# Moving the second look at layer 0's weights from layer 1 to block 1 of layer 0, with layer 1's first tiles loaded behind it

## The chip, the cores and the metric

One core of a Trainium2 chip runs the program. The metric is the device time of one execution in microseconds (us). TensorE (PE) multiplies matrices, VectorE (DVE) and ScalarE (ACT) do the elementwise work, GpSimd (POOL) a little of it, and SyncE (SP) issues all the DMAs of this program in one queue. Each engine runs its instructions in the order in which they stand in its own list, and waits at an instruction until what it depends on is there.

## The reference

Attention with sink tokens and a window, then two feed-forward layers, each with its own weights, which come as 64-bit floats:

```python
def _moe_ref(x, w_in, w_out):            # layer 0
    h = x @ w_in                          # [1536, 512] @ [512, 2048]
    sp = np.where(h > 20.0, h, np.log1p(np.exp(np.minimum(h, 20.0))))
    return (h * np.tanh(sp)) @ w_out      # [1536, 2048] @ [2048, 512]

def _moe2_ref(x, w_in, w_out):           # layer 1
    h = x @ w_in
    return (h * np.clip(h + 3.0, 0.0, 6.0) / 6.0) @ w_out

def reference(...):
    x = attention(q, k, v, n_sink, window)    # [2, 8, 768, 64] -> [1536, 512]
    return _moe2_ref(_moe_ref(x, ...), ...)
```

## The kernel before

The 1536 tokens are 12 units of 128, grouped into three blocks of four (`BLOCKS`). Attention for the first two blocks is computed ahead and beside layer 0's first steps; attention for the third block (units 8 to 11, `last`) runs as side work beside layer 0's block 1. The matmuls of the layers run in steps. In layer 0 a step takes two of the 16 slices f of the hidden dimension for one block: `up` multiplies the input by w_in into h (24 matmuls of 512 columns, two halves), a chain on ScalarE and VectorE makes the activation, and `down` multiplies by w_out (24 matmuls). `down` comes one step late (`LAG = 1`). Every value is kept as a high and a low float16 half: the chain ends with the high half of g on ScalarE (L748) and the low half on VectorE (L749), whose input e VectorE writes just before (L744). In order, layer 0 runs block 0 (stage 0), block 1 (stage 1) and block 2 (stage 2), eight steps each; layer 1 follows with steps of four slices, multiplied by Strassen's scheme in `up2` and `down2`.

Weights come in 16 tiles for each layer. `fetch_w` loads one tile (w_in and w_out parts, 512 KB each) into `raw`, of which there are two buffers (`STB = 2`). `gen_decode` turns a tile into float16 halves: on VectorE two operations into y (L210, L211), one into p (L212), then splits (L250, L268) and, for a pair of layer 1's tiles, four sums t (L260 to L263). y has one buffer. Layer 0's 16 tiles are decoded in stage 0, layer 1's in stage 2 and at the start of layer 1, a pair in most steps (`PAIRS`). When a tile's y and p are made, `load_w` fetches the next tile in the sequence `wseq` (layer 0's, then layer 1's), so two tiles are always ahead.

The second look (`gen_check`) loads layer 0's tiles once more, two ahead, and for each one masks the exponents on VectorE (`exponents`, L184) and sums them on ScalarE (L188). The sums only serve the test, at the end, of whether the fast path was allowed.

The pieces of side work (attention, decoding, look) are handed out by `hook`, four times in a step. A scheduler then orders the instructions of each engine, and may move them ahead where it expects their inputs; a look is marked to keep its place. Setting `budget["chk"]`, `CHECK = 7` lets the look begin at the eighth stage, in layer 1, once `raw_t` is empty, that is when all of layer 1's tiles are decoded. In the loop over steps, before stage 2, `att_side.until` hands out what is left of attention, and `open_second` frees attention's buffers and takes them for layer 1's.

Of the kernel before, what the change touches and what calls it, by code (L numbers as in the profile page):

```python
# [29 lines left out]
def attention_moe_moe2(  # L30
# [13 lines left out]
    nc = tc.nc  # L44
# [4 lines left out]
    KF = DFF // 128  # L49
# [109 lines left out]
    wseq = [(layer, f) for layer in range(2) for f in range(KF)]  # L159
    wsrc = ((w1_in, w1_out), (w2_in, w2_out))  # L160
    nload = [0]

    def fetch_w(layer, f):
        wi, wo = wsrc[layer]
        t = st_p.tile([128, 2, 512, 2], I32, tag="raw", name="raw")
        nc.sync.dma_start(
            out=t[:, 0].rearrange("p (k f) t -> p k (f t)", k=KD),
            in_=wi[:, f * 256:(f + 1) * 256].rearrange("(k p) f -> p k f", p=128),
        )
        nc.sync.dma_start(out=t[:, 1].rearrange("p f t -> p (f t)"), in_=wo[f * 128:(f + 1) * 128, :])  # L170
        return t

    def load_w():
        if nload[0] >= len(wseq):
            return
        layer, f = wseq[nload[0]]
        nload[0] += 1
        raw_t[layer, f] = fetch_w(layer, f)

    def exponents(idx, t, pin=False):  # L180

        y = dec_p.tile([128, 1024], I32, tag="y", name="y").bitcast(I16)[:, 0:1024]
        top = t.rearrange("p f t -> p (f t)").bitcast(I16).rearrange("p (f t) -> p f t", t=4)[:, :, 3]
        look = nc.vector.tensor_scalar(out=y, in0=top, scalar1=0x7800, scalar2=0x3800, op0=ALU.bitwise_and, op1=ALU.bitwise_xor)  # L184
        if pin:
            tc.keep_in_program_order(look)
        yy = y.bitcast(I32)
        nc.scalar.activation(out=yy, in_=yy, func=AF.Copy, accum_out=wchk[:, idx:idx + 1])  # L188

    def gen_check():  # L190


        ahead = []
        for f in range(KF + 2):
            if f > 1:
                exponents(f - 2, ahead.pop(0).rearrange("p a f t -> p (a f) t"), True)
            if f < KF:
                ahead.append(fetch_w(0, f))
            yield
            yield  # L200

    def gen_decode(idx):
        layer, f = wseq[idx]
        t = raw_t.pop((layer, f)).rearrange("p a f t -> p (a f) t")
        halves = t.rearrange("p f t -> p (f t)").bitcast(I16).rearrange("p (f t) -> p f t", t=4)
        y = dec_p.tile([128, 1024], I32, tag="y", name="y")
        yh = y.bitcast(I16).rearrange("p (f t) -> p f t", t=2)
        p = (late["p"] if layer == 1 else dec_p).tile([128, 1024], I32, tag="p", name="p")

        nc.vector.tensor_scalar(out=yh[:, :, 1], in0=halves[:, :, 3], scalar1=-0x800, scalar2=-0x800, op0=ALU.bitwise_and, op1=ALU.bitwise_xor)  # L210
        nc.vector.tensor_scalar(out=yh[:, :, 0], in0=halves[:, :, 1], scalar1=13, scalar2=7, op0=ALU.logical_shift_right, op1=ALU.bitwise_and)  # L211
        nc.vector.scalar_tensor_tensor(out=p, in0=t[:, :, 1], scalar=3, in1=y, op0=ALU.logical_shift_left, op1=ALU.bitwise_xor)  # L212
        if layer == 1:
            yf = y.bitcast(F32)
            nc.scalar.activation(out=yf, in_=yf, func=AF.Square, accum_out=wchk[:, idx:idx + 1])  # L215
        pf = p.bitcast(F32).rearrange("p (a f) -> p a f", a=2)
        load_w()
        if layer == 1:
            yield from split_pair(f, pf)
            return  # L220
        w = (w_a if f < KF // 2 else late["w_b"]).tile([128, 2, 2, 512], F16, tag="w", name="w")
        nc.scalar.activation(out=w[:, :, 0, :], in_=pf, func=AF.Copy, scale=2.0 ** SW)
        yield
        nc.vector.scalar_tensor_tensor(out=w[:, :, 1, :], in0=pf, scalar=2.0 ** SW, in1=w[:, :, 0, :], op0=ALU.mult, op1=ALU.subtract)
        wt[layer, 0, f] = w[:, 0]
        wt[layer, 1, f] = w[:, 1]
        if f == 0:
            watch(w[:, 0, 0, 0:64])
            watch(w[:, 1, 0, 0:64])
# [235 lines left out]
    def open_second():  # L465

        p2.close()
        late["p"] = main.enter_context(tc.tile_pool(name="p_b", bufs=2))
        late["g7"] = main.enter_context(tc.tile_pool(name="g7", bufs=2 * (LAG + 1)))
        late["w_c"] = main.enter_context(tc.tile_pool(name="w_c", bufs=WC))  # L470
# [235 lines left out]
    att_side = Side(gen_units())  # L706
    dec_side = Side(gen_weights())
    chk_side = Side(gen_check())


# [3 lines left out]
    def per_bank(blk):  # L714
        return 512 // (len(blocks[blk]) * 128)
# [109 lines left out]
    def down2(st, span):  # L825
        layer, blk, f = st
        g2 = gt.pop(st)
        fa, fb = span
        if f == fa:
            acc[layer, blk] = [ps_acc.tile([128, 2, 256], F32, tag="acc", name="acc") for _ in range(4)]  # L830
        a = acc[layer, blk]
        for m in range(2):
            first, last = f + 2 * m == fa, f + 2 * m == fb - 2
            wp = wt[1, 1, f // 2 + m]
            for i in range(NP):
                g, w = g2[m][i], wp[i]
                for x, (l_, r_) in enumerate(((g[:, 0], w[:, 0]), (g[:, 0], w[:, 1]), (g[:, 1], w[:, 0]))):

                    nc.tensor.matmul(a[i // 2][:, i % 2], l_, r_, start=first and i % 2 == 0 and x == 0, stop=last and x == 2 and (i % 2 == 1 or i == NP - 1), skip_group_check=True)  # L839
            hook()  # L840
        if f + 4 == fb:
            finish2(blk, [a[i // 2][:, i % 2] for i in range(NP)], span)
# [61 lines left out]
    load_first(first[1], "v")  # L904
    load_first(first[2])
    load_w()
    load_first(first[3])
    for _ in range(STB - 1):
        load_w()
# [24 lines left out]
    def moe_steps():  # L934
        pend = []
        fmax = n2 = 0
        for s, (cur, span) in enumerate(steps):
            layer, j, f = cur
            fend = layer * KF + f + (2 * per_bank(j) if layer == 0 else 4)
            stage = STAGES.index((layer, j) + span)  # L940
            budget["chk"] = stage >= CHECK and not raw_t
            if f == span[0] and layer == 0 and j >= 2:
                att_side.until(("unit", blocks[j][-1]))
                open_second()
            budget["att"] = RATES[stage]
            if layer == 0 and j < 2:
                fmax = max(fmax, fend)
                budget["lim"] = 2 * min(fmax + AHEAD[stage], KF)
            else:

                budget["lim"] = 2 * (KF + 2 * PAIRS[n2])
                n2 += 1
            dec_side.until(("dec", fend - 1))
            (up if layer == 0 else up2)(cur)
            yield
            pend.append((cur, span))
            while len(pend) > LAG:
                x = pend.pop(0)
                (down if x[0][0] == 0 else down2)(*x)
        for x in pend:  # L960
            down2(*x)

    moe = moe_steps()
    first_blocks()
    p1.close()
# [181 lines left out]
NATG = 2  # L1147
STAGES = [(0, 0, 0, 16), (0, 1, 0, 16), (0, 2, 0, 16)]
STAGES += [(1, (j, h), fa, fa + 8) for fa in (0, 8) for j in (0, 1) for h in (0, 1)] + [(1, (2, h), 0, 16) for h in (0, 1)]
CHECK = 7  # L1150
WC = 8
PAIRS = [1, 2, 3, 4, 4, 5, 6, 6, 7] + [8] * 100
LAG = 1
STB = 2
# [42 lines left out]
```

## Time and profile before

| | |
|---|---|
| time, median of 3 runs | 605.94 us (605.9 to 606.38) |
| the profiled execution: its time, its span | 606.01 us, 604.2 us |
| TensorE busy over the span | 580.9 us (96%) |
| VectorE busy | 458.7 us (76%) |
| ScalarE busy | 398.0 us (66%) |
| DMA, share of 16 engines, moved | 41.9%, 71.48 MB |
| granted TensorE clock, mean | 0.995 |

Shares over the whole span hide the stages. The first matmul of block 1's first step starts at 162.4 us, that of block 2 at 265.9, that of layer 1 at 352.2. A row of the trace in order of time gives the start, the duration, the engine, the line, the operation with its output and inputs, and in brackets how long the engine was idle before and what ended that.

### The profile page before, as it was taken

The numbers are of one execution on the slowest core, as the hardware profiler recorded it, in microseconds if no ns is written. First come the engines' busy times: TensorE is split into PE (matmuls) and PEld (weight loads), VectorE is DVE, ScalarE is ACT, GpSimd is POOL, SyncE is SP. The second block draws the span as 40 slices with busy tenths as digits, with TensorE's granted clock in tenths as the row PEclk, the third lists the DMA queues.
The fourth block names the chain that finished last, engine by engine and source line by source line (L and its number), as shares of the span: only waits on it lengthen the run. The fifth ranks groups of instructions, "written<-read, shape, count | busy, mean of one in ns | idle before, by whom it ended". The sixth has DMA issues, their size and how long they took to land.

```text
span 604.2 us, 11390 instructions
## 1 busy us (share of the span) xinstructions
PE 580.9 (96%) x4424; PEld 395.6 (65%) x4424; DVE 458.7 (76%) x1104; ACT 398.0 (66%) x786; POOL 24.9 (4%) x36
## 2 busy tenths in 40 slices
PE   8999999999989999899999999999999999999992
PEld 5778764444445545444434468888888888888882
DVE  5788999989375554589999999766678888956662
ACT  5998787778687776679788876433445565534441
POOL 0130100700000000000000000000000000000000
PEclk9999999999999999999999999999999999999997
DMA  9867257998234433253534432000026767100001
GB/s 184 217 127 244 75 207 196 212 264 227 88 72 88 82 62 61 43 159 133 210 139 157 154 109 71 1 1 2 1 92 224 246 216 268 75 1 1 36 2 41
DMA packets 105846, 72.28 MB, mean 120 GB/s; under 512 B 73512, under 2 KB 98088, under 8 KB 105784
## 3 DMA queue, kind: packets, MB, share of 16 engines
q1 hardware_dynamic: 105784, 71.48, 41.9%
q8 instruction: 36, 0.59, 0.4%
q14 instruction: 26, 0.21, 0.1%
HBM read 60.43 MB, written 3.15 MB: 105 GB/s over the span
## 4 chain that ended last, share of the span: by engine, by line
PE 59%; DVE 14%; ACT 11%; issue 10%; DMA 2%; POOL 2%; SPq 1%; DVEq 0%; ACTq 0%; POOLq 0%
PE acc L839 18%; PE h L803 7%; PE h L802 7%; PE h L801 7%; PE acc L777 6%; PE h L732 3%; PE h L734 2%; PE h L733 2%; DVE p L212 2%; ACT e L740 2%; ACT e L741 2%; DVE d L352 2%; DVE g L749 2%; PE o L391 2%; ACT y L215 1%
## 5 line engine op out<-in xcount | busy, mean ns | idle before, releaser
L777 PE MATMUL acc<-g,w 128*128 128x512 f16 x576 | 131.3, 379 | 4.1 <-DVE g L749 3.7
L839 PE MATMUL acc<-w,g 128*128 128x256 f16 x1008 | 113.8, 273 | 0.0
L839 PEld LDWEIGHTS <-g 128*128 128x128 f16 x1008 | 98.6, 98 | 11.4
L802 PE MATMUL h<-xt,w 128*128 128x256 f16 x384 | 104.7, 273 | 0.0
L801 PE MATMUL h<-xt,w 128*128 128x256 f16 x384 | 104.7, 273 | 0.0
L803 PE MATMUL h<-xt,w 128*128 128x256 f16 x384 | 104.7, 273 | 0.0
L777 PEld LDWEIGHTS <-w 128*128 128x128 f16 x576 | 55.4, 98 | 70.0 <-issue 5.7
L732 PE MATMUL h<-xt,w 128*128 128x512 f16 x192 | 72.8, 379 | 2.8 <-DVE mins L553 2.2
L734 PE MATMUL h<-xt,w 128*128 128x512 f16 x192 | 72.8, 379 | 0.0
L733 PE MATMUL h<-xt,w 128*128 128x512 f16 x192 | 72.8, 379 | 0.0
L806 DVE SCALAR_TENSOR_TENSOR e<-e,h 128x512 f32<-128x512 f32 x48 | 32.8, 684 | 41.3 <-ACT e L805 41.3
L805 ACT ACTIVATE e<-h,bias 128x512 f32<-128x512 f32 x48 | 32.5, 677 | 45.8 <-PE h L803 45.8
L818 ACT ACTIVATE g<-sm 128x512 f16<-128x512 f32 x48 | 30.3, 631 | 29.4 <-DVE sm L813 28.9
L818 ACT ACTIVATE g<-e 128x256 f16<-128x256 f32 x96 | 29.5, 355 | 28.7 <-DVE e L806 28.1
L819 DVE SCALAR_TENSOR_TENSOR g<-sm,g 128x512 f16<-128x512 f32 x48 | 33.0, 688 | 12.8 <-ACT g L818 12.8
L744 DVE SCALAR_TENSOR_TENSOR e<-e,h 128x512 f32<-128x512 f32 x48 | 30.8, 680 | 15.3 <-ACT e L742 15.1
L801 PEld LDWEIGHTS <-w 128*128 128x128 f16 x384 | 37.6, 98 | 4.5
L802 PEld LDWEIGHTS <-w 128*128 128x128 f16 x384 | 37.6, 98 | 4.5
L803 PEld LDWEIGHTS <-w 128*128 128x128 f16 x384 | 37.6, 98 | 4.4
L735 ACT ACTIVATE e<-h 128x512 f32<-128x512 f32 x48 | 28.2, 589 | 17.2 <-PE h L734 17.2
L212 DVE SCALAR_TENSOR_TENSOR p<-raw,y 128x1024 int32<-128x1024 int32 x32 | 39.1, 1222 | 0.3
L749 DVE SCALAR_TENSOR_TENSOR g<-e,g 128x1024 f16<-128x1024 f32 x24 | 29.3, 1222 | 8.3 <-ACT g L748 8.3
(172 smaller groups left out, 937.7 us busy)
## 6 DMA issues: line engine op xcount, KB each, us to landing
raw<-in_moe_w_in_dram SPq DMA_DIRECT2D x48, 512.0 KB, 3.9
raw<-in_moe_w_out_dram SPq DMA_DIRECT2D x48, 512.0 KB, 4.7
out_dram<-ob SPq DMA_DIRECT2D x12, 256.0 KB, 2.1
first<-in_k_dram SPq DMA_DIRECT2D x8, 256.0 KB, 4.8
first<-in_q_dram SPq DMA_DIRECT2D x8, 256.0 KB, 4.8
first<-in_v_dram SPq DMA_DIRECT2D x8, 256.0 KB, 3.3
nk<-in_k_dram SPq DMA_DIRECT2D x5, 256.0 KB, 5.5
nv<-in_v_dram SPq DMA_DIRECT2D x5, 256.0 KB, 6.3
```

What stands on the lines that cost most here:

```text
L212: nc.vector.scalar_tensor_tensor(out=p, in0=t[:, :, 1], scalar=3, in1=y, op0=ALU.logical_shift_left, op1=ALU.bitwise_xor)
L732: nc.tensor.matmul(o, wh, x[:, 0, c, :], start=c == 0, stop=False)
L733: nc.tensor.matmul(o, wh, x[:, 1, c, :], start=False, stop=False)
L734: nc.tensor.matmul(o, wl, x[:, 0, c, :], start=False, stop=c == KD - 1)
L749: nc.vector.scalar_tensor_tensor(out=gl, in0=e, scalar=sc, in1=gh, op0=ALU.mult, op1=ALU.subtract)
L777: nc.tensor.matmul(o, l_, r_, start=first and m == 0 and x == 0, stop=last and end and x == 2, skip_group_check=True)
L801: nc.tensor.matmul(o, wh, x[:, 0, c, :], start=c == 0, stop=False)
L802: nc.tensor.matmul(o, wh, x[:, 1, c, :], start=False, stop=False)
L803: nc.tensor.matmul(o, wl, x[:, 0, c, :], start=False, stop=c == KD - 1)
L818: nc.scalar.activation(out=g[:, 0, d_], in_=src, func=AF.Copy, scale=sc)
L819: nc.vector.scalar_tensor_tensor(out=g[:, 1, d_], in0=src, scalar=sc, in1=g[:, 0, d_], op0=ALU.mult, op1=ALU.subtract)
L839: nc.tensor.matmul(a[i // 2][:, i % 2], l_, r_, start=first and i % 2 == 0 and x == 0, stop=last and x == 2 and (i % 2 == 1 or i == NP - 1 ...
```

## The change

Four edits belong together. `CHECK = 0` lets the look begin as soon as `raw_t` is empty; `load_w` stops behind layer 0's last tile until `checked` holds something; so `raw_t` is empty when block 0 has decoded layer 0, and the look's 16 tiles are fetched and looked at from block 1's hooks, two tiles a step. Before block 2, behind the last of attention, what is left of the look is handed out, `checked` is set, and the first two tiles of layer 1 are fetched. `fetch_w` gets a `queue` argument, which is SyncE everywhere.

```diff
     nload = [0]
-
-    def fetch_w(layer, f):
+    checked = []
+
+    def fetch_w(layer, f, queue=nc.sync):
...
     def load_w():
-        if nload[0] >= len(wseq):
+        if nload[0] >= (len(wseq) if checked else KF):
             return
...
             if f < KF:
-                ahead.append(fetch_w(0, f))
+                ahead.append(fetch_w(0, f, nc.sync))
...
                 att_side.until(("unit", blocks[j][-1]))
+                while chk_side.piece():
+                    pass
+                checked.append(True)
+                for _ in range(STB):
+                    load_w()
                 open_second()
...
-CHECK = 7
+CHECK = 0
```

In the changed file most of these lines stand one further down (the look L185, decoding L211 to L213, e L745, g L750, x L649, loads L167 and L171).

VectorE before, from g of block 1's seventh step on (x is the last attention unit's output, raw and y belong to tiles of layer 1):

```order
L749 SCALAR_TENSOR_TENSOR g_2985<-e,g_2985 128x1024
L648 TENSOR_TENSOR x_3031<-xf,x_3031 128x512
L210 TENSOR_SCALAR y<-raw 128x1024
L211 TENSOR_SCALAR y<-raw 128x1024
L260 TENSOR_TENSOR t<-p 128x256
L212 SCALAR_TENSOR_TENSOR p<-raw,y 128x1024
L261 TENSOR_TENSOR t<-p,t 128x256
L262 TENSOR_TENSOR t<-p 128x256
L263 TENSOR_TENSOR t<-t,p 128x256
L210 TENSOR_SCALAR y<-raw 128x1024
L211 TENSOR_SCALAR y<-raw 128x1024
L250 SCALAR_TENSOR_TENSOR w<-p,w 128x512
```

The e of block 1's last step stands five rows further on. So two of layer 1's tiles, and the third one's y, are ahead of it.

VectorE in the change, from the same g (here g_3063) on; L185 is the look:

```order
L750 SCALAR_TENSOR_TENSOR g_3063<-e,g_3063 128x1024
L649 TENSOR_TENSOR x_3109<-xf,x_3109 128x512
L185 TENSOR_SCALAR y<-raw 128x1024
L745 SCALAR_TENSOR_TENSOR e<-e,h 128x512 x2
L750 SCALAR_TENSOR_TENSOR g_3169<-e,g_3169 128x1024
L185 TENSOR_SCALAR y<-raw 128x1024
L211 TENSOR_SCALAR y<-raw 128x1024
L212 TENSOR_SCALAR y<-raw 128x1024
L213 SCALAR_TENSOR_TENSOR p<-raw,y 128x1024
L261 TENSOR_TENSOR t<-p 128x256
L211 TENSOR_SCALAR y<-raw 128x1024
```

The last two looks stand beside the e and g of block 1's last step (g_3169), and layer 1's first tile is decoded behind them.

VectorE in the change, at block 1's sixth step:

```order
L185 TENSOR_SCALAR y<-raw 128x1024
L645 TENSOR_TENSOR xf<-o,ri 128x512
L649 TENSOR_TENSOR x_2929<-xf,x_2929 128x512
L185 TENSOR_SCALAR y<-raw 128x1024
L745 SCALAR_TENSOR_TENSOR e<-e,h 128x512 x2
L750 SCALAR_TENSOR_TENSOR g_2909<-e,g_2909 128x1024
```

Before, the rows at this place are the same without the two looks: xf, x, e, g.

SyncE in the change, at the end of block 1 (atg and xt2 are transposes of attention, moe2 are layer 1's weights):

```order
L578 DMA_TRANSPOSE atg_3005<-ag_3004 128x17x128
L167 DMA raw_3014<-in_moe_w_in_dram 128x4x256
L171 DMA raw_3014<-in_moe_w_out_dram 128x1024
L167 DMA raw_3115<-in_moe_w_in_dram 128x4x256
L171 DMA raw_3115<-in_moe_w_out_dram 128x1024
L651 DMA_TRANSPOSE xt2_90<-x16_3109 128x8x128
L167 DMA raw_3199<-in_moe2_w_in_dram 128x4x256
L171 DMA raw_3199<-in_moe2_w_out_dram 128x1024
L167 DMA raw_3202<-in_moe2_w_in_dram 128x4x256
L171 DMA raw_3202<-in_moe2_w_out_dram 128x1024
```

Before, this stretch has one load (layer 1's third tile) between the last atg and the last xt2; now the look's last two loads stand there, and layer 1's first two come behind xt2.

## Rows read from the trace of the kernel before

**Rows 1.** Busy us (x instructions) by stage; clock, DMA share, GB/s.
```profile
162.40:265.90 103.50, 99.81 (x762) 49.84 (x761) 59.77 (x134) 76.45 (x137) 0.30 (x1) 1.00 0.39 82
...
265.90:352.20 86.30, 83.74 (x386) 37.48 (x385) 81.83 (x123) 75.11 (x109) 0.00 (x0) 1.00 0.42 147
...
352.20:392.00 39.80, 39.80 (x343) 33.39 (x342) 36.63 (x97) 23.22 (x48) 0.00 (x0) 1.00 0.17 54
...
441.00:510.00 69.00, 69.00 (x635) 61.84 (x633) 58.66 (x160) 38.78 (x98) 0.00 (x0) 1.00 0.61 212
```

**Rows 2.** TensorE around its waits: start us, duration us, instruction.
```profile
242.27 0.38 PE L777 MATMUL acc<-g,w 128*128 128x512 f16 x1 [0.88 <-DVE g L749]
...
281.54 1.67 PE L777 MATMUL acc<-g,w 128*128 128x512 f16 x7
...
304.29 1.02 PE L777 MATMUL acc<-g,w 128*128 128x512 f16 x4 [1.35 <-DVE g L749]
...
337.06 1.24 PE L777 MATMUL acc<-g,w 128*128 128x512 f16 x5 [0.98 <-DVE g L749]
```

**Rows 3.** Groups by shape, 441-525: busy us, mean ns | idle before.
```profile
L184 DVE TENSOR_SCALAR y<-raw 128x1024 int16<-128x1024 int16 x16 | 11.0, 687 | 0.0
...
L188 ACT ACTIVATE y<-y 128x512 int32<-128x512 int32 x16 | 10.0, 627 | 1.6 <-DVE y L184 1.6
```

**Rows 4.** DMA issues: KB each, median us from issue to landing.
```profile
raw<-in_moe_w_out_dram SPq DMA_DIRECT2D x48, 512.0 KB, 4.7
```

**Rows 5.** VectorE in order of time, block 1 and block 2.
```profile
238.52 1.28 DVE L744 SCALAR_TENSOR_TENSOR e<-e,h 128x512 f32<-128x512 f32 x2 [0.26 <-ACT e L742]
...
266.71 1.28 DVE L744 SCALAR_TENSOR_TENSOR e<-e,h 128x512 f32<-128x512 f32 x2
...
279.52 1.22 DVE L749 SCALAR_TENSOR_TENSOR g<-e,g 128x1024 f16<-128x1024 f32 x1
...
303.04 1.21 DVE L749 SCALAR_TENSOR_TENSOR g<-e,g 128x1024 f16<-128x1024 f32 x1
```

**Rows 6.** VectorE's groups by shape, 266 to 352 us.
```profile
L212 DVE SCALAR_TENSOR_TENSOR p<-raw,y 128x1024 int32<-128x1024 int32 x13 | 15.9, 1221 | 0.2
L744 DVE SCALAR_TENSOR_TENSOR e<-e,h 128x512 f32<-128x512 f32 x16 | 10.2, 678 | 0.4 <-ACT e L742 0.3
L749 DVE SCALAR_TENSOR_TENSOR g<-e,g 128x1024 f16<-128x1024 f32 x8 | 9.7, 1216 | 0.0
L210 DVE TENSOR_SCALAR y<-raw 128x1024 int16<-128x1024 int16 x12 | 9.1, 754 | 1.9 <-ACT y L215 1.9
L211 DVE TENSOR_SCALAR y<-raw 128x1024 int16<-128x1024 int16 x12 | 9.0, 746 | 0.0
L268 DVE SCALAR_TENSOR_TENSOR w<-t,w 128x1024 f16<-128x1024 f32 x7 | 8.5, 1221 | 1.6 <-ACT w L267 1.6
L250 DVE SCALAR_TENSOR_TENSOR w<-p,w 128x512 f16<-128x512 f32 x12 | 8.2, 682 | 0.2 <-ACT w L249 0.2
L268 DVE SCALAR_TENSOR_TENSOR w<-p,w 128x512 f16<-128x512 f32 x6 | 4.1, 683 | 0.0
L268 DVE SCALAR_TENSOR_TENSOR w<-p,w 128x256 f16<-128x256 f32 x7 | 3.0, 422 | 1.4 <-ACT w L267 1.2
...
L260 DVE TENSOR_TENSOR t<-p 128x256 f32<-128x256 f32 x6 | 2.5, 419 | 0.1
```

**Rows 7.** ScalarE in order of time, input of block 1's last chain.
```profile
260.88 0.60 ACT L735 ACTIVATE e<-h 128x512 f32<-128x512 f32 x1
```

**Rows 8.** Both engines in order of time, layer 1.
```profile
381.85 0.69 DVE L819 SCALAR_TENSOR_TENSOR g<-sm,g 128x512 f16<-128x512 f32 x1 [0.49 <-ACT g L818]
...
387.47 2.78 PE L839 MATMUL acc<-w,g 128*128 128x256 f16 x24
```

**Rows 9.** SyncE's queue in order of time, last x transpose of block 2.
```profile
257.00 1.24 SPq L650 DMA_TRANSPOSE xt<-x  x1
```

**Rows 10.** Who waited for whom, whole span: us in total, times, longest.
```profile
DVE y L210 <- DMA raw<-in_moe_w_out_dram: 2.8, 4, 1.7
```

More of the change, by code (lines that the diff above doesn't have):

```diff
@@ L161, in attention_moe_moe2 @@
     nload = [0]
-    def fetch_w(layer, f):
+    checked = []
+    def fetch_w(layer, f, queue=nc.sync):
         wi, wo = wsrc[layer]
         t = st_p.tile([128, 2, 512, 2], I32, tag="raw", name="raw")
-        nc.sync.dma_start(
+        queue.dma_start(
             out=t[:, 0].rearrange("p (k f) t -> p k (f t)", k=KD),
@@ L169, in fetch_w @@
         )
-        nc.sync.dma_start(out=t[:, 1].rearrange("p f t -> p (f t)"), in_=wo[f * 128:(f + 1) * 128, :])
+        queue.dma_start(out=t[:, 1].rearrange("p f t -> p (f t)"), in_=wo[f * 128:(f + 1) * 128, :])
         return t
     def load_w():
-        if nload[0] >= len(wseq):
+        if nload[0] >= (len(wseq) if checked else KF):
             return
```

## The prediction

> **What bounds the kernel now.** I read the busy time by stage first, then the single gaps of TensorE, then the order of the instructions around the edit. The first view [rows 1] cuts the span where the stages change. In 441 to 510 us, where most of the second look runs today, TensorE is busy 69.00 of 69.00 us. In layer 0's block 1 (162.4 to 265.9) it is busy 99.81 of 103.5 us, VectorE only 59.77, ScalarE 76.45. In block 2 (265.9 to 352.2) VectorE is busy 81.83 of 86.3 us: it decodes layer 1 there, and TensorE loses time to it. At the start of layer 1 (352.2 to 392) VectorE is busy 36.63 of 39.8, TensorE without a gap. The gaps themselves stand in [rows 2]: TensorE waited 1.35 us before 304.29 and 0.98 us before 337.06 for the low half of g from VectorE, and 0.88 us before 242.27 in block 1. So block 2 is balanced between two engines, and what VectorE gets extra there is paid by TensorE.
>
> **What is removed.** Sixteen looks leave layer 1. Each is 0.687 us on VectorE and 0.627 us and an accumulator read on ScalarE [rows 3], 11.0 us of VectorE in all. With TensorE at 69.00 of 69.00 us there, the price of their removal is 0.0 us of gain. Their 32 loads leave that stretch too, and nothing waits for a DMA there.
>
> **What block 1 gets.** Sixteen looks and loads, in the 43.7 us that VectorE and the 27 us that ScalarE have free there [rows 1]. The generator fetches each tile two looks ahead. The second half of a tile lands 4.7 us after its issue [rows 4], and by the order of the queues its look comes some 6 to 15 us after it, so I take no wait for the loads, with about 1 us of margin at the tightest places. The cost is then that of a look which stands in front of a late chain. The tight chain is the one for which TensorE already waits at 242.27: there the order now puts a look between x and the chain's e. In today's trace VectorE idles 0.26 us between these two [rows 5], so 0.69 us of look pushes e, and with it g, by about 0.35 us. At the other steps the same walk leaves TensorE covered, by 0.2 us at the least. Term: +0.35 us; bounds 0 and 16 x 0.687 = 11 us if every look fell on a tight chain; I take the low end since VectorE is 58% busy.
>
> **What block 2 loses.** Today layer 1's first two tiles are loaded long before, and VectorE decodes them in the last 12 us of block 1; the order shows both, and the third tile's y, ahead of the e of block 1's last step. In the changed order nothing of layer 1 is decoded before that step's g. A pair of tiles costs VectorE 2 x (0.754 + 0.746 + 1.221 + 0.682) + 4 x 0.418 + 1.221 + 0.683 + 0.422 = 10.8 us [rows 6]. With the third tile's y, that is about 12 us of work moved out of free time into a stretch where VectorE has 86.3 - 81.83 = 4.5 us free, and 39.8 - 36.63 = 3.2 us at the start of layer 1.
>
> I follow it step by step, counting over the two order lists how much decoding stands between successive g's of block 2. Today it is 5.8, 7.6, 12.1, 8.4, 7.5, 10.4, 6.1, 8.5 us; changed it is 7.2, 8.5, 10.8, 10.8, 9.1, 6.1, 6.9, 10.8 us (durations of [rows 6]). To each step 2 x 0.678 + 1.216 us for e and g are added, and these durations overlap a little. Today's walk from g at 279.52 to g at 303.04 [rows 5] takes 23.5 us for 19.7 us of decoding, 5.1 us of e and g and 0.7 of a finish, so I multiply by 0.92.
>
> The start: block 1's last e stands at 266.71 today, because its ScalarE chain, whose input is ready at 260.88 + 0.60 [rows 7], has decoding between its parts. In the changed order nothing is between them, so e comes at about 265 and g ends near 268.7. The last look follows, 0.69 us, and only its end frees the buffer of layer 1's second tile, so that load is issued at about 269.4 and is there at about 269.4 + 0.4 + 4.7 = 274.5. Tile one was issued behind the last x and is there. VectorE decodes tile one from about 270.3, waits about 1.3 us for tile two, and the first g of block 2 ends near 282.5 (today 279.52 + 1.22 = 280.7). TensorE asks for it from 281.54 [rows 2]: about 1.0 us late. From there, with the eight sums: second g at 294.0 against 292.1 + 1.0, another 1.0 late; third at 306.3 against 304.29, so 2.1 late in all; fourth 318.6, 4.0 late; fifth 329.3, 4.3 late; the sixth step has 4.3 us less decoding than today, so today's wait of 0.98 us before 337.06 and a little beside it vanish and 2.8 stays; the last two fit. Term: +2.8 us. Bounds: 0 if the 4.5 us of free time take it all; 12 - 4.5 + 1.3 = 8.8 us if nothing gives way.
>
> **Start of layer 1.** The changed order has 9.7 us more decoding than today's in the first two and a half steps of layer 1, where it catches up. The cover is the lag of one step: a g that VectorE ends at 381.85 + 0.69 is wanted half of 4.5 us (one step's 42 matmuls) behind 387.47 [rows 8], 7.2 us later. 9.7 x 0.92 = 8.9 us against 7.2 us and about 1 us of gaps: I take +1.0 us, bounds 0 and 4. After that TensorE is full to the end, so no delay is won back.
>
> **Sum.** The profiled execution took 606.01 us (span 604.2, 1.8 around it), as the median of 605.94. 606.0 - 0.0 + 0.35 + 2.8 + 1.0 = 610.1 us (rounded down).
>
> **The rivals.**
> Nothing measurable (604.7 to 607.2): VectorE's free 4.5 + 3.2 us and the lag of a step soak up the shift; only the 0.35 and a part of the first wait stay, 606.0 + 0.5 = 606.5 us. For it speaks that today's order also ran late in block 2 and kept its 7 us of cover at layer 1; against it that TensorE had no cover left before 304.29 and 337.06. The Trainium skill (Perfetto Trace Analysis, section Optimization Strategy) says that a kernel whose most contended engine changes over time may gain from interleaving its regimes. By that rule the move is free or better, since it takes work for VectorE to a block in which VectorE is 58% busy; the busy shares of block 1 agree, but the rule does not see what is pushed on into block 2, and by it alone the sum would be 606.0.
>
> Faster: the last chain of block 1 is freed from decoding (2.7 us earlier), and step six lightens. If the wait for the second tile does not bite, the waits of 1.35 and 0.98 us go and nothing takes their place: 606.0 - 2.3 = 603.7 us. It decides if the first g of block 2 ends before 281.5 and the third before 302.6. Against it: the third g needs 2 us that the sums don't give.
>
> Much slower: the SyncE queue is in order, and in the changed one each load stands behind a transpose that waits for VectorE. The last x transpose of block 2 (issued at 257.00 today, [rows 9]) is now behind two loads of 1 MB. If the loads took 9 us in place of 5 beside the transposes, looks would stall VectorE and block 2's first matmuls would wait for x: at 2 us for each of four tight looks, 606.0 + 4.1 + 8 = 618 us. Against so much speak today's loads beside transposes in block 0: over the whole span VectorE waited 2.8 us for them, in four pieces of at most 1.7 us [rows 10]. The Trainium skill (DMA: Bandwidth & Descriptors, section Queues, rings and completion order) says that descriptors of one issuing engine are consumed in ring order, which puts that last transpose behind both loads. By that rule and 5 us a load it would land near 262, before block 2's first matmul at 265.9; no row of this trace shows a transpose behind two loads.
>
> **How the numbers follow.** About 0.2% (1.2 us) is what a measurement of this kernel can tell from no change. My forecast, 607.2 to 614, has a chance of 0.57; nothing measurable 0.20; faster 0.09; much slower 0.14. The bounds of the three terms would allow 606 to 630, but their ends are not reached together; 605.5 to 615 leaves out some 0.1 on each side. Faster 0.09, same 0.20, slower 0.71.
>
> **What would show it.** The profile of the changed kernel should show 16 looks of about 0.69 us between 165 and 270 us; layer 1's steady steps unchanged at 9.8 us; block 1 longer by under 1.5 us; block 2 longer by 2 to 4 us, with TensorE's waits for g in its first five steps and VectorE over 95% busy; a wait of VectorE of 1 to 2 us for the second raw tile near 273. Wrong would be: waits of VectorE for raw in block 1 of several us in sum (the DMA rival); block 2 no longer than 86.3 us; or a gain in layer 1, which I put at zero.

## The result, and the profile after

The changed kernel takes 612.08 us (median of 5 runs, 610.31 to 613.2), the kernel before 605.94 beside it (605.41 to 606.38). The ratio is 1.0096, 95% interval 1.0073 to 1.012: slower by about 1%. The forecast was 610.1, with 605.5 to 615 as its range. The profiled execution has a span of 610.3 us, before 604.2.

The windows by stage, which answer to [rows 1] (busy us and instructions of PE, PEld, which is TensorE's loading of weights, DVE, ACT, POOL, then granted clock as a share of full speed, DMA share, GB/s):

```profile
161.60:266.10 104.50, 99.72 (x762) 49.95 (x761) 60.98 (x136) 80.84 (x160) 0.29 (x1) 1.00 0.82 211
266.10:351.70 85.60, 84.08 (x385) 37.52 (x384) 80.90 (x125) 73.06 (x106) 0.00 (x0) 1.00 0.46 160
351.70:388.20 36.50, 35.51 (x302) 29.34 (x300) 35.83 (x79) 25.23 (x49) 0.00 (x0) 1.00 0.18 59
388.20:391.70 3.50, 0.26 (x3) 0.00 (x0) 3.49 (x14) 2.03 (x5) 0.00 (x0) 0.96 0.00 0
391.70:397.80 6.10, 6.06 (x42) 4.84 (x43) 5.97 (x21) 2.43 (x6) 0.00 (x0) 0.74 0.00 0
441.00:510.00 69.00, 69.00 (x634) 61.85 (x633) 51.59 (x146) 30.37 (x70) 0.00 (x0) 1.00 0.05 17
```

Ahead of block 1 this execution is 0.8 us shorter than the one of before. Block 1 is 1.0 us longer, block 2 is 0.7 us *shorter*, and from 441 us on TensorE is as full as before although VectorE lost 7 us of work there. The time went at layer 1's start: a hole at 388 us (3.5 us in this cut), with VectorE full, and behind it a stretch at a granted clock of 0.74. The same cut for all kernels of this study, from the starts of the first matmul of each stage in the traces (the last column runs to the end of the span). The times are medians, but the stages of each row are of one profiled execution; that of hold_gpsimd took 615.83 us, that of after_spread 607.0, of after_even 606.21 and of after_no_look 609.45:

| kernel | median us | ratio to before (95%) | block 1 | block 2 | layer 1 |
|---|---|---|---|---|---|
| before | 605.94 | | 103.45 | 86.30 | 252.08 |
| changed | 612.08 | 1.0096 (1.0073 to 1.012) | 104.50 | 85.65 | 258.57 |
| late_tiles | 612.78 | 1.0115 (1.0101 to 1.013) | 103.26 | 87.77 | 258.54 |
| early_look | 621.35 | 1.0267 (1.0238 to 1.0296) | 120.71 | 85.75 | 251.78 |
| after_hold | 605.24 | 1.0004 (0.9995 to 1.0014) | 103.57 | 85.66 | 252.88 |
| after_no_look | 610.21 | 1.0081 (1.0068 to 1.0094) | 102.92 | 88.17 | 254.18 |
| up_pinned | 610.47 | 1.008 (1.0066 to 1.0093) | 103.47 | 87.77 | 256.05 |
| hold_gpsimd | 620.34 | 1.0263 (1.024 to 1.0285) | 114.97 | 85.67 | 251.48 |
| after_spread | 606.01 | 1.0009 (1.0 to 1.0018) | 104.91 | 84.94 | 253.47 |
| before_spread | 606.62 | 1.0028 (1.0016 to 1.0039) | 103.35 | 85.69 | 253.47 |
| before_even | 605.6 | 1.0003 (0.9994 to 1.0012) | 103.47 | 86.43 | 252.02 |
| after_even | 605.39 | 1.0001 (0.9991 to 1.0011) | 105.02 | 86.11 | 251.72 |

The kernel before ran beside each group of the later kernels, at 605.18 to 605.29 us. Line numbers of the changed kernel are one higher than in the rows of before; in the other kernels they are up to five higher, in after_no_look lower.

First VectorE at the seam of block 1 and block 2 (order of time: start, duration, instruction, idle time before it):

```profile
265.19 1.28 DVE L745 SCALAR_TENSOR_TENSOR e<-e,h 128x512 f32<-128x512 f32 x2 [7.34 <-ACT e L743]
...
268.80 0.69 DVE L185 TENSOR_SCALAR y<-raw 128x1024 int16<-128x1024 int16 x1
...
274.57 0.76 DVE L211 TENSOR_SCALAR y<-raw 128x1024 int16<-128x1024 int16 x1 [1.20 <-DMA raw<-in_moe_w_out_dram]
...
280.92 1.22 DVE L750 SCALAR_TENSOR_TENSOR g<-e,g 128x1024 f16<-128x1024 f32 x1
...
304.88 1.22 DVE L750 SCALAR_TENSOR_TENSOR g<-e,g 128x1024 f16<-128x1024 f32 x1
```

VectorE stands idle for 7.34 us before block 1's last e, where it used to decode; then come the last look, and a wait of 1.20 us for the second tile of layer 1. The third g of block 2 ends at 306.10, which is 1.9 us later than in [rows 5]. TensorE over the same third g:

```profile
303.85 0.38 PE L733 MATMUL h<-xt,w 128*128 128x512 f16 x1
304.50 1.02 PE L778 MATMUL acc<-g,w 128*128 128x512 f16 x4 [0.27 <-ACT g L749]
305.36 0.38 PE L734 MATMUL h<-xt,w 128*128 128x512 f16 x1
...
306.01 0.38 PE L734 MATMUL h<-xt,w 128*128 128x512 f16 x1
306.22 0.38 PE L778 MATMUL acc<-g,w 128*128 128x512 f16 x1
```

In [rows 2] it stood still for 1.35 us here. Now it runs four matmuls that need only the high half of g, then four of the next step's up, and by then the low half is there: 0.27 us of idle time. Last, VectorE where layer 1's first finished half-block is summed (L854, `finish2`; before it is L853), in the kernel before:

```profile
382.46 2.20 DVE L853 TENSOR_TENSOR ob<-acc,ob 128x256 f32<-128x256 f32 x6
```

and in the changed one, with TensorE's answer from its own timeline:

```profile
384.63 1.22 DVE L269 SCALAR_TENSOR_TENSOR w<-t,w 128x1024 f16<-128x1024 f32 x1
385.77 1.02 DVE L269 SCALAR_TENSOR_TENSOR w<-p,w 128x256 f16<-128x256 f32 x2
...
389.65 0.42 DVE L854 TENSOR_TENSOR ob<-acc,ob 128x256 f32<-128x256 f32 x1
...
390.84 1.74 DVE L854 TENSOR_TENSOR ob<-acc,ob 128x256 f32<-128x256 f32 x5
```

```profile
391.74 1.65 PE L840 MATMUL acc<-w,g 128*128 128x256 f16 x7 [3.28 <-DVE ob L854]
```

The sums read the accumulators that the next `down2` writes. Decoding that was over at 375 us before now ends at 386.8 and pushes the sums from 382.46 to 389.65; TensorE waits 3.28 us for its accumulators.

### The profile page after: what moved, and what is told of

Read it like the earlier page. It is cut to its first block, busy times and chain, and to the rows that moved or that the text cites. A ratio compares the mean times of both kernels' runs of the same rounds, so it can differ in the third digit from the quotient of the medians.

```text
span 610.3 us, 11375 instructions
## 1 busy us (share of the span) xinstructions
PE 582.4 (95%) x4424; PEld 395.9 (65%) x4424; DVE 457.9 (75%) x1104; ACT 397.1 (65%) x786; POOL 25.3 (4%) x36
## 4 chain that ended last, share of the span: by engine, by line
PE 52%; DVE 23%; ACT 13%; DMA 5%; issue 4%; SPq 1%; POOL 0%; DVEq 0%; ACTq 0%; POOLq 0%
PE acc L840 17%; PE h L804 6%; PE h L803 6%; PE h L802 6%; PE acc L778 5%; DVE p L213 3%; PE h L733 3%; PE h L734 3%; PE h L735 2%; DVE g L750 2%; DMA atg<-ag 2%; ACT e L741 2%; DVE e L745 2%; DVE y L212 2%; DVE w L269 2%
## 5 line engine op out<-in xcount | busy, mean ns | idle before, releaser
L840 PE MATMUL acc<-w,g 128*128 128x256 f16 x1008 | 115.3, 275 | 3.3 <-DVE ob L854 3.3
L745 DVE SCALAR_TENSOR_TENSOR e<-e,h 128x512 f32<-128x512 f32 x48 | 30.8, 683 | 20.7 <-ACT e L743 20.7
L213 DVE SCALAR_TENSOR_TENSOR p<-raw,y 128x1024 int32<-128x1024 int32 x32 | 39.2, 1224 | 0.2
L750 DVE SCALAR_TENSOR_TENSOR g<-e,g 128x1024 f16<-128x1024 f32 x24 | 29.4, 1224 | 8.5 <-ACT g L749 8.5
```

The lines of the kernel that those rows point to most:

```text
L745: nc.vector.scalar_tensor_tensor(out=e[:, i], in0=e[:, i], scalar=2.5, in1=hps[i], op0=ALU.subtract, op1=ALU.mult)
L750: nc.vector.scalar_tensor_tensor(out=gl, in0=e, scalar=sc, in1=gh, op0=ALU.mult, op1=ALU.subtract)
```

## The experiments

Theory A: the late first tiles put VectorE's decoding one pair behind, and the debt is paid at layer 1's start. Rival B: the looks and their loads themselves cost.

**late_tiles.** The kernel before, with its looks left where they were:

```diff
+    opened = []
...
-        if nload[0] >= len(wseq):
+        if nload[0] >= (len(wseq) if opened else KF):
...
                 att_side.until(("unit", blocks[j][-1]))
+                for _ in range(STB):
+                    t = st_p.tile([128, 2, 512, 2], I32, tag="raw", name="raw")
+                    tc.keep_in_program_order(nc.vector.memset(t[:, 0, 0:1, 0], 0))
+                opened.append(True)
+                for _ in range(STB):
+                    load_w()
                 open_second()
```

> The kernel before with its looks left in layer 1; only layer 1's first two tiles come late: their two buffers are held until the end of block 1 by a one-element memset each. Theory A (late tiles): the order of VectorE in block 2 becomes that of the changed kernel, some 12 us of decoding are carried on to the start of layer 1, and TensorE waits there about 3 us near 388 us for the sums of the first finished half-block and then runs at the lower clock for about 3 us; 610 to 612 us. Rival B (the looks and their loads in block 1 are what costs): there are none here, so 605.5 to 606.8 us.

It took 612.78 us. Its waits of TensorE between 345 and 400 us (us in total, times, longest) are close to those of the changed kernel, where they are 3.3 and 1.0:

```profile
PE acc L840 <- DVE ob L854: 2.7, 1, 2.7
PE acc L778 <- DVE g L750: 1.4, 1, 1.4
```

Without one look moved, a loss of this size is there, and layer 1 is as long as in the changed kernel (258.54 us). Theory A holds, and B is not needed. The tiles come later still than in the changed kernel, because both loads wait for the end of block 1; VectorE begins to decode at

```profile
273.21 0.76 DVE L211 TENSOR_SCALAR y<-raw 128x1024 int16<-128x1024 int16 x1 [5.32 <-DMA raw<-in_moe_w_out_dram]
```

in place of 270.27, and block 2 is 1.5 us longer than before. So the run shows that late tiles are enough for such a loss, and not that each us of the changed kernel's is theirs.

**early_look.** The changed kernel with the look handed out twice as fast (the loop that empties the look before block 2 goes, and layer 1's first loads with it):

```diff
-        if budget["chk"]:
-            chk_side.piece()
+        if budget["chk"] and not checked:
+            for _ in range(2):
+                if not chk_side.piece():
+                    checked.append(True)
+                    for _ in range(STB):
+                        load_w()
+                    break
```

> The changed kernel with two pieces of the look per hook, so that the look ends some 30 us before block 1 does, and layer 1's first tiles are loaded as soon as it has ended. All 16 looks and their loads still stand in block 1. Theory A (late tiles): VectorE decodes two tiles in block 1 again, no wait near 388 us, 605.4 to 606.8 us. Rival B (the looks cost): they stand closer than before, at least what the changed kernel lost, 610 us or more.

It took 621.35 us, outside A's figure, and yet layer 1 lost nothing (251.78 us, no wait for the sums). All of it is in block 1, 120.71 us long. TensorE's waits there, the loads, and the whole block in the columns of the first windows:

```profile
PE s L547 <- DMA qt<-q: 4.0, 1, 4.0
PE o L624 <- DMA atg<-ag: 2.9, 2, 2.0
PE s L547 <- DVE mins L554: 2.6, 3, 1.4
```

```profile
raw<-in_moe_w_out_dram SPq DMA_DIRECT2D x18, 512.0 KB, 6.8
```

```profile
162.30:283.00 120.70, 107.13 (x762) 52.88 (x761) 71.50 (x153) 86.59 (x170) 0.56 (x1) 0.94 0.78 209
```

At this density the loads land after 6.8 us (4.9 in block 1 of the changed kernel), TensorE waits for transposes of attention, and VectorE waits 9.9 us in eight pieces for raw tiles. TensorE's granted clock fell as well: its mean in block 1 is 0.94 (last row), in the changed kernel 1.00, and 0.06 x 120.7 = some 7 us is an estimate of what that cost. The look as a term is small only at the pace of the changed kernel; this run cures layer 1 and breaks block 1, so it speaks for A on layer 1 alone.

**after_no_look.** The look's work left out, its loads and raw buffers kept (y, which a look uses too, is not taken by it here):

```diff
-        look = nc.vector.tensor_scalar(out=y, in0=top, scalar1=0x7800, scalar2=0x3800, op0=ALU.bitwise_and, op1=ALU.bitwise_xor)
...
-        nc.scalar.activation(out=yy, in_=yy, func=AF.Copy, accum_out=wchk[:, idx:idx + 1])
+        tc.keep_in_program_order(nc.vector.memset(t[:, 0:1, 0], 0))
...
```

> The changed kernel with the second look's arithmetic left out: its 32 loads and the order in which buffers are released stay, but each look is a memset of one element and nothing runs on ScalarE for it (the exponents of layer 0 are not looked at, so this part of the computation is left out). Theory A: late tiles remain, so 610.0 to 612 us, with block 1 about 0.3 to 1 us shorter. Rival B (16 looks of 0.69 us and 0.63 us in block 1 cost): near 606.5 us.

610.21 us: a loss stays without the looks' arithmetic. It lies in other places than in the changed kernel: block 2 is 1.9 us longer than before (88.17 us), layer 1 2.1 us (254.18). Block 1 is 102.92 us long, 1.6 less than with it in the changed kernel and 0.65 less than in after_hold, which has the same looks.

**after_hold.** The changed kernel with its last four tiles held back (`first` is the first operation of a tile's y, here pinned to its place in VectorE's order; `PAIRS` says how many pairs may be handed out by each step):

```diff
+        if idx >= KF + 12:
+            tc.keep_in_program_order(first)
...
-                budget["lim"] = 2 * (KF + 2 * PAIRS[n2])
+                budget["lim"] = int(2 * (KF + 2 * PAIRS[n2]))
...
-PAIRS = [1, 2, 3, 4, 4, 5, 6, 6, 7] + [8] * 100
+PAIRS = [1, 2, 3, 4, 4, 5, 6, 6, 6, 6.5, 6.5, 7, 7, 7.5, 7.5] + [8] * 100
```

> The changed kernel with the last four tiles of layer 1 decoded one at a time over the first eight steps of layer 1 (the first instruction of each is pinned to its place), block 2 as it is. Theory A: the sums of the first finished half-block no longer stand behind a pair's decoding, the wait of 3.3 us and the lower clock behind it go, 5.0 to 5.5 us in all, and about 0.4 us is left of the first g of layer 1's start: 606.0 to 607.2 us. Rival: VectorE is too full there, and the wait comes back one or two steps later, 609 us or more.

605.24 us, the time of before. Block 2 is the changed kernel's (85.66 us), but VectorE reaches the sums at once (first row), and TensorE's only wait from 345 to 590 us is the second:

```profile
381.45 2.20 DVE L856 TENSOR_TENSOR ob<-acc,ob 128x256 f32<-128x256 f32 x6
```

```profile
PE acc L780 <- DVE g L752: 0.4, 1, 0.4
```

So the loss is in the place of the decoding in layer 1's first steps, not in its amount. All 16 looks and their loads still stand in block 1 here, and it is 103.57 us long, before 103.45: rival B is out as the main cause.

**up_pinned.** The changed kernel with TensorE held to strict turns of up and down in block 2:

```diff
-                    nc.tensor.matmul(o, wh, x[:, 0, c, :], start=c == 0, stop=False)
+                    mm = nc.tensor.matmul(o, wh, x[:, 0, c, :], start=c == 0, stop=False)
+                    if blk == 2 and m == c == 0:
+                        tc.keep_in_program_order(mm)
```

> The changed kernel with the first matmul of each half of up in block 2 pinned behind everything written before it on TensorE, so that up and down take turns strictly there, as in the kernel before; in the changed kernel four pieces of a later up stand between the first 4 and the other 20 matmuls of a down. Theory A1 (this order of TensorE hid block 2's late g's): TensorE now waits for the low half of g in the first five steps, block 2 is 2 to 4 us longer than the 85.6 us of the changed kernel, and since VectorE catches up meanwhile the wait near 388 us shrinks by about as much: 610 to 613 us in all. Rival A2 (the g's of block 2 are not late enough to matter): block 2 within 1 us of 85.6, the wait near 388 us unchanged. Rival A3 (nothing is given back): 614 us or more.

610.47 us. TensorE's timeline at the third g, and at the sums:

```profile
303.69 1.02 PE L780 MATMUL acc<-g,w 128*128 128x512 f16 x4 [1.13 <-ACT g L751]
305.34 1.02 PE L780 MATMUL acc<-g,w 128*128 128x512 f16 x4 [0.62 <-DVE g L752]
...
390.77 5.49 PE L842 MATMUL acc<-w,g 128*128 128x256 f16 x34 [2.11 <-DVE ob L856]
```

Block 2 is 2.1 us longer than in the changed kernel, layer 1 2.5 us shorter: A1. Together they take 343.82 us, in the changed kernel 344.22. What TensorE waits in block 2 VectorE catches up with, and in this run it is not waited for again.

**hold_gpsimd.** after_hold with `fetch_w(0, f, nc.gpsimd)` for the look's loads.

> The changed kernel with the last four tiles held back (605.24 us), and the look's 32 loads issued from GpSimd's queue in place of SyncE's. If the loads cost block 1 something because transposes stand behind them in SyncE's queue, block 1 gets shorter by up to 1 us (it was 104.5 us beside 103.5 us before the change): 604.2 to 605.0 us. Rival (the loads cost by the bandwidth they take, or nothing): 605.0 to 606 us.

620.34 us, wrong on both accounts: block 1 grew to 114.97 us in the profiled execution, the fastest of the five (615.83 us). ScalarE's timeline shows the first place. Below it stand the DMA queues from 160 to 277 us (packets, MB, share), and last the one queue of after_hold from 160 to 265 us:

```profile
175.39 0.63 ACT L526 ACTIVATE q<-nq 128x512 f16<-128x512 f32 x1 [2.83 <-DMA qt<-q]
```

```profile
q0 software_dynamic: 4032, 14.68, 37.9%
q1 hardware_dynamic: 25616, 7.31, 34.3%
```

```profile
q1 hardware_dynamic: 35024, 21.99, 79.9%
```

In after_hold the same q follows without a gap, at 171.95. There the load of that moment is issued behind the transpose, at 168.53; here GpSimd issues it at 167.66, beside the transpose that SyncE issues at 167.63, and the transpose lands later. So at this place SyncE's order, which I had counted as a danger, keeps the load behind the transposes. A part of the 11.4 us is the clock's: its mean in block 1 is 0.97, in after_hold 1.00, which makes some 0.03 x 115 = 3 us (an estimate).

**after_spread, before_spread, after_even, before_even.** Can VectorE's work be handed out so that block 2's waits go as well? The spread kernels pin every tile of layer 1 from the third on and use `PAIRS = [1, 2, 2, 3, 4, 4, 5, 5.5, 5.5, 6, 6, 6.5, 6.5, 7, 7, 7.5] + [8] * 100`; the even ones pin the sums too and hand out portions of a pair (`PIECES`, in quarters of a pair, 32 behind the last that is listed), before_even with `[7, 9, 12, 15, 17, 20, 23, 24, 24, 25, 27, 28, 28, 29, 31, 31]`, after_even with `[3, 7, 9, 12, 15, 17, 20, 21, 23, 24, 25, 27, 28, 29, 31, 31]`.

> The changed kernel with layer 1's decoding spread over block 2 and the first eight steps of layer 1 (five and a half pairs in block 2 in place of all but one and a half, each tile pinned to its place). Theory A (VectorE's debt is what costs): TensorE's waits for g in block 2, 1.4 us, go too, and no wait near 388 us: 603.3 to 605.0 us, faster than both kernels. Rival: VectorE is too full in layer 1's first steps, waits for g or for the sums come back there, 606 us or more.

> The kernel before, its look still in layer 1, with the same spreading of layer 1's decoding. Theory A: the waits of 1.35 and 0.98 us in block 2 go: 603.3 to 604.5 us. If the look has to leave layer 1 for this (VectorE too full with both), it is 605.5 us or more and slower than the changed kernel with the same spreading.

> The kernel before, its look in layer 1, with layer 1's decoding handed out evenly: two of the three portions of a pair (3.4, 3.4 and 4.0 us) in each step of block 2, one in its last, none in the first step of layer 1 and the other six over the next eight, each portion pinned to its place. Theory A (the waits of 1.35 and 0.98 us in block 2 come from uneven steps): they go and layer 1 stays at 252.1 us: 603.3 to 604.6 us. Rival (VectorE is full over the whole stretch, evenness moves the waits only): 604.9 to 606.5 us.

> The changed kernel with the same even handing out, one pair behind: two portions a step from the first step of block 2, one in each of the first steps of layer 1. Theory A: no wait near 388 us, block 2 under 85 us, 604.0 to 605.5 us. Rival (with the pair that came late there is too much for VectorE before the first sums): a wait for the sums or for layer 1's first g, 606 us or more.

None beats both kernels: 606.01, 606.62, 605.6 and 605.39 us. after_spread gains 1.4 us in block 2 and before_spread 0.6, and both give 1.4 back in layer 1 (253.47 us). The even ones gain nothing in block 2 (86.11 and 86.43 us); after_even's time is inside A's figure, but by layer 1 (251.72 us), not by block 2 as A had it. So evenness only moves the waits, as the rivals said. Block 1 is over 1.3 us longer in after_spread and after_even than in after_hold, which has the same looks there. TensorE waits no more than there, but its clock falls (last section). With the decoding well placed, the look's place makes no difference that this measurement can tell (after_hold, after_even).

## Why the prediction was right, and where its sum was not

The direction, the cause (layer 1's first tiles come late, and VectorE carries a pair of decoding along as a debt) and the total were right; the debt was put in the wrong place. One sign that the prediction named for being wrong did come: block 2 is no longer than 86.3 us.

- *Removal from layer 1, 0.0 us.* Right: 69.00 of 69.00 us before and after.
- *Block 1, +0.35 us.* 104.50 against 103.45 us in this profile, but 103.57 in after_hold and 103.47 in up_pinned with the same looks, so 0.0 to 1.1 where the clock held. The tight chain came out worse than forecast: TensorE waits there 0.64 us for the high half of g and 0.89 for the low half, in place of 0.88 in all, and it waits less at other places. The changed kernel's profile has one wait more than after_hold's, for attention's `mins` (first row; second row after_hold); why, the two profiles don't show.

```profile
PE s L547 <- DVE mins L554: 2.1, 2, 1.1
PE s L549 <- DVE mins L556: 0.9, 1, 0.9
```

- *The seam.* Forecast: e near 265, g's end 268.7, the load issued at 269.4, tile two there at 274.5, a wait of 1.3 us, first g at 282.5. Measured: 265.19, 268.88, 269.51, 274.57, 1.20, 282.14.
- *Block 2, +2.8 us.* Wrong: -0.65. VectorE's walk was right (next g's forecast 294.0, 306.3, 318.6, 329.3, measured 293.66, 306.10, 318.01, 328.50). The step that failed is "TensorE asks for it" at the times of [rows 2]: I took TensorE's order from the trace of before, while in the changed kernel four matmuls on the high half and a part of the next up stand ahead of those that need the late half. TensorE's idle time for g in block 2 is 1.4 us in five pieces, against 2.3 us before (rows below). up_pinned shows the difference: with strict turns block 2 is 87.77 us, 1.5 above before, which is still only half of the 2.8.

```profile
PE acc L778 <- DVE g L750: 0.9, 3, 0.4
PE acc L778 <- ACT g L749: 0.5, 2, 0.3
```

- *Layer 1's start, +1.0 us, bounds 0 and 4.* Wrong: 258.57 against 252.08, so +6.5, beyond the bound. The debt was roughly of the right size: 8.9 us forecast, and the sums are 389.65 - 382.46 = 7.2 us late. What failed is the cover, "7.2 us": that is the cover of g. The sums that free the accumulators had 387.47 - (382.46 + 2.20) = 2.8 us, with which the prediction's own sum would have been 8.9 - 2.8 - 1 = 5.1 us. The wait for them is 3.28 us. The first down in layer 1 waits another 0.99 us for g. The third part was in no term: the 42 matmuls behind the hole start over 5.96 us (391.74 to 397.70) in place of 4.48 in [rows 8]'s step (387.47 to 391.95), so the lower clock costs 1.5 us. These make 5.8. From start to start of matmuls the two waits cost 3.55 and 1.15 us, since the end of a matmul, from which idle time counts, is modelled; that makes 6.2 in all, and 0.3 us is spread over the rest of the stage.

That the total came within 2 us is partly luck: the two errors had opposite signs (-3.5 and +5.5 us), and 1.5 us of the second is a fall of the clock that no term had. Since up_pinned shows that the debt is paid once, in whichever stage TensorE first feels it, the sum was safer than its parts; but in late_tiles, where the tiles come later still, both stages lose. The rival with loads and transposes did not occur at this pace; early_look, at twice the pace, shows it, with 17 us in block 1, the clock's part among them.

## What to carry to other kernels

A delay on a full engine travels until some deadline is tight; look for every deadline there, the release of an accumulator as well as the result itself, and take the smallest cover. Read the new order of the engine that waits too: it may fill the hole that you count. When work is moved, also ask which load it holds back: here it was not the looks that cost 1%, but the two load buffers that they kept until the end of block 1, and a better place for four tiles won it back.

## What was not expected of the hardware

TensorE's granted clock fell after some short holes and not after others. In the changed kernel TensorE was idle for 3.28 us up to 391.74, and then (first fence, columns as in the first windows above) ran at 0.50, its 1.2 GHz level, until about 395; after_no_look had a hole of 2.14 us up to 391.02 and stayed at 1.00 (second fence); up_pinned with 2.11 us fell again, its next 42 matmuls starting over 6.09 us.

```profile
392.00:393.00 1.00, 1.00 (x7) 0.67 (x6) 1.00 (x3) 0.00 (x0) 0.00 (x0) 0.50 0.00 0
```

```profile
391.00:392.00 1.00, 0.98 (x9) 0.90 (x10) 1.00 (x4) 0.00 (x0) 0.00 (x0) 1.00 0.00 0
392.00:393.00 1.00, 1.00 (x12) 0.89 (x10) 1.00 (x4) 0.50 (x2) 0.00 (x0) 1.00 0.00 0
```

Block 1 shows it with equal holes. In after_hold (first two rows) and after_spread (last two) TensorE waits 0.64 us and then 0.88 us for the two halves of the same g. In after_hold the clock stays at 1.00. In after_spread it falls to 0.50 for about 3 us, and so it does in after_even; their blocks 1 are 1.3 and 1.5 us longer than after_hold's:

```profile
241.41 0.59 PE L780 MATMUL acc<-g,w 128*128 128x512 f16 x2 [0.88 <-DVE g L752]
243.00:244.00 1.00, 1.00 (x7) 0.41 (x5) 0.09 (x1) 0.97 (x5) 0.00 (x0) 1.00 0.13 53
241.90 0.59 PE L780 MATMUL acc<-g,w 128*128 128x512 f16 x2 [0.88 <-DVE g L752]
243.00:244.00 1.00, 1.00 (x4) 0.36 (x3) 0.28 (x2) 1.00 (x5) 0.00 (x0) 0.50 0.60 225
```

It may also differ between executions of one kernel: two of up_pinned's six had a mean clock of 0.995 and 0.996 and took 609.12 and 608.62 us, the other four 0.992 to 0.993 and 610.34 to 611.02. Only one execution of each kernel has a profile, so that these two had no fall at 391 us is not shown. What decides whether the clock falls, no run here shows.

Moving loads to a second queue made block 1 11.4 us longer (hold_gpsimd, 114.97 against 103.57). Its packets there are 14.68 MB / 4032 = 3.6 KB each, those of the other queue 7.31 MB / 25616 = 0.3 KB. The move also changed the loads themselves: SyncE's queue lost 35024 - 25616 = 9408 packets with the same 14.68 MB (1.6 KB each), so the loads went from 9408 packets to 4032. Which of the two, the second queue or the larger packets, made the transposes late, no run here separates. The Trainium skill (DMA: Bandwidth & Descriptors, section Queues, rings and completion order) says that a DMA engine takes turns between queues packet by packet; by that rule a queue of small packets gets fewer bytes per turn beside one of large packets. The direction agrees with the run; neither the turns nor whether the profile's packets are those of the page does any row here show.
